# A gated mix of attention and a spectral filter on one core: the first unit's queries, keys and values are evicted into attention's own tiles

## The chip, the cores and the metric

The kernel runs on one core of a Trainium2 chip. The metric is the device time of one execution in microseconds (us). Three executions of the kernel before took 444.52, 444.55 and 444.66 us; their median, 444.55 us, is the time that the change is measured against. The core's engines each run their own list of instructions in order: PE (matrix products), DVE, ACT and POOL (elementwise work), and SP, which here only issues transfers. ACT and POOL issue transfers as well.

## The reference

The input x has 2048 positions of 640 numbers. Three things are computed from it and mixed:

```python
g = sigmoid((x * gate_w).sum(-1, keepdims=True))
# a: 32 heads of 20 numbers; position s sees positions s, s-2, ..., s-14
q, k, v = x @ wqkv, split by head
logits = q[s] . k[s - 2*w] * 20**-0.5      (w = 0..7, -1e9 before the first position)
a = (softmax(logits) weighted v) @ wo
# b: a filter in the frequency domain
b = irfft2(rfft2(x) * (w_r + 1j * w_i))
out = g * a + (1 - g) * b
```

All numbers are fp32.

## The kernel before

**Layout.** The 2048 positions lie as 128 partitions of 16 positions each (position 16p + j). Since attention reaches back in steps of two, even j (parity 0) and odd j (parity 1) are independent, and each has eight positions (jj = 0 to 7) in a partition. Position jj of a partition needs the seven positions of its parity before it, so the first seven rows that a partition uses come from the partition in front of it.

**Units.** The 32 heads go in four groups of eight, and a unit is one parity with one group: unit u = 4 * parity + group, each with 480 columns of queries, keys and values, in six blocks of 80 columns (four heads each; a and b are the two halves of a unit). The function `qkv` makes a unit: for each jj, 15 matmuls on PE (three products of split numbers over five chunks of the depth) fill one PSUM bank out of four; ACT evicts the bank with a copy of 480 columns into a tile `ev`, and for group 0 one more column into `z` for the gate; after every second jj, `store_rows` sends the pair to the tensor `qkvd` in main memory on ACT's queue. In unit 0 the weights' columns are in the order that `key_rows` undoes (query a, key a, query b, key b, value a, value b).

**Attention.** For half a unit, `fetch` loads keys (15 rows of 80, `kt`, 7 of them from the partition in front) and queries (`q`, 8 rows) from `qkvd`, and `attend` loads the values (`vt`, 15 rows). In main memory a partition's rows follow those of the partition in front, so one load of 15 rows per partition brings the overlap with it; rows before the first position were zeroed by `zero_rows`. `products` then has ACT copy two query rows into a PSUM third (`qbank`), DVE multiply them with eight keys each (`pr`) and DVE reduce them into logits (`L`); one of four such steps is on POOL except in the first units. Softmax follows on DVE, POOL and ACT, `weigh` multiplies with values on POOL (`pv`), and DVE reduces them into outputs (`o`), which go to main memory (`od`). The order of half units is 0a, 0b, 4a, 4b, 1a, 1b, 2a and so on (UNITS); the names in the trace carry that number (`pr0a`, `kt4b`).

**The filter.** `fold` turns x (`fx`) into its sums and differences by ACT, DVE or POOL; four of the eight are stored to main memory (`fd`) by ACT's queue and loaded again later. `cols` and `freq` transform (`z`, then groups of frequencies in pairs, in the order GORD = 1, 2, 3, 0, 4, ...; group 0 is special and has tables of its own, `tbfirst`), multiply with the filter and transform back (`g`, `xa`, `xc` on PE, `ab`, `xd`, `s`, `p` on DVE). `spatial`, `project_even` and `project_odd` make the output: transforms `oa` to `od`, `ha`, `hb`, and the products with wo (`woa`, `wob`).

**The order.** All calls are first recorded as a list with their dependences. A planner in the kernel file gives each a modelled length and makes an order by list scheduling forward and backward (`turns`); `order` repeats this for a list of random seeds, STEPS, each of which shakes the priorities in a part of the span. The instructions are then issued in that order, so each engine's list is fixed. Every operation is recorded by a helper, which is why all rows of the trace name the same line, L681; they are told apart by their tiles.

Of the kernel before, what the change touches and what calls it, by code (L numbers as in the profile page):

```python
# [16 lines left out]
S, D = 2048, 640  # L17
NJ = 16
HD = 20
GORD = (1, 2, 3, 0) + tuple(range(4, 16))  # L20
GC = 160
HC = 80
ROWS = 7 + 1024
# [4 lines left out]
BQ, BF = (0, 1, 2, 3), (4, 5, 6)  # L28
# [121 lines left out]
class Plan:  # L150
# [311 lines left out]

    def issue(self, tc):
        order = self.order()
        with tc.manual_schedule():
            for op in order:
                exec(*op.call)
# [29 lines left out]
)  # L497
ENGS = ("PE", "DVE", "ACT", "POOL", "SP")
BEGIN = {"PE": 0.8, "DVE": 0.5, "ACT": 0.5, "POOL": 0.5, "SP": 0.5}
ISSUE = {"SP": 0.45, "ACT": 0.42, "POOL": 1.15}  # L500
LAG = {"PE": 0.27, "DVE": 0.14, "ACT": 0.16, "POOL": 0.15}
PACKETS, RATE, LAND, LANES = (0.52e-3, 2.3e-6), 345e3, (2.3, 1.9), 8
# [36 lines left out]
class Mixer:  # L539
# [17 lines left out]
    def places(self, pp, dr, sb):  # L557
# [13 lines left out]
        def ring(*tags):  # L571
            return Ring(sb, *tags)

        def n(tag, k):
            return ring(*(f"{tag}{i}" for i in range(k)))
# [6 lines left out]
        self.evrs = {0: ring("ev0", "ev1", "pr0", "pr1"), 4: ring("e0", "e1", "ev0", "ev1")}  # L582
        self.xor = ring("raw0", "raw1", "raw2", "raw3", "raw4", "kv4", "kv5", "ya")

        self.vsr, self.mdr, self.wpr = ring("raw2"), ring("mm", "ev0", "ev1"), n("f", 3)
# [3 lines left out]
        self.wor, self.war, self.yar = ring("ya", "e1", "raw1"), ring("w2", "w3", "w4", "w0", "w1", "w5", "w6"), ring("ya")  # L589
# [13 lines left out]
    def work(self):  # L603
        p, ins = self.p, self.ins
        S = p.sp
# [16 lines left out]
        self.fetched, self.ahead = {}, None  # L622
        self.qkv(0, 0)
# [123 lines left out]
    def store_rows(self, src, u, block, jj):  # L747
        n, k = src.shape[1], src.shape[2]
        d = self.qkv_d
        to = bass.AP(  # L750
            tensor=d.tensor,
            offset=d.offset + ((6 * u + block) * ROWS + 7 + jj) * HC,
            ap=[[8 * HC, 128], [ROWS * HC, n], [1, k * HC]],
        )
        self.p.act.dma_start(to, src.rearrange("p i j c -> p i (j c)"))

    def terms_qkv(self, j, hg, c0, c1, whole):
        hi, lo = self.xT[j]
        terms = []
        for t in (0, 2, 1, 4, 3) if whole else range(5):  # L760
            x = slice(128 * t, 128 * t + 128)
            if whole:
                terms.append((self.xraw[j][:, x], self.wraw[hg, t][:, c0:c1]))
            else:
                terms += [(a[:, x], w[hg][t][:, c0:c1]) for a, w in ((hi, self.wh), (hi, self.wl), (lo, self.wh))]
        return terms

    def first_keys(self):

        p = self.p  # L770
        n = 2 * HC
        kept = self.one("ev_first", 2, 8, HC, tag="pr1")
        done = 0
        for jj in range(8):
            b = self.ps(BQ, f"qk0_{jj}")
            terms = self.terms_qkv(2 * jj, 0, 0, n, jj == 0)
            for i, (a, w) in enumerate(terms):
                p.pe.matmul(b[:, 0:n], a, w, start=(i == 0), stop=(i == len(terms) - 1))
            p.act.copy(kept[:, :, jj], b[:, 0:n].rearrange("p (i c) -> p i c", i=2))
            if jj in FIRST_STORES:  # L780
                self.store_rows(kept[:, :, done : jj + 1], 0, 0, done)
                done = jj + 1

    def qkv(self, par, hg, between=None):
        p = self.p
        u = 4 * par + hg
        b0 = 0
        c0, n = b0 * HC, 480 - b0 * HC
        for jj in range(8):
            j = 2 * jj + par  # L790
            b = self.ps(BO if u == 7 and jj > 3 else BQ, f"qkv{u}_{jj}")
            terms = self.terms_qkv(j, hg, c0, 482 if hg == 0 else 480, j == 0 and hg == 0)
            for i, (a, w) in enumerate(terms):
                p.pe.matmul(b[:, 0 : w.shape[1]], a, w, start=(i == 0), stop=(i == len(terms) - 1))
            if jj % 2 == 0:
                ev = self.evrs.get(u, self.evr).next(f"ev{u}_{jj}", 6, 2, HC)
            p.act.copy(ev[:, b0:, jj % 2], b[:, 0:n].rearrange("p (i c) -> p i c", c=HC))
            if hg == 0:
                p.act.copy(self.z[:, j : j + 1], b[:, n : n + 1])
            if jj % 2:  # L800
                self.store_rows(ev[:, b0:], u, b0, jj - 1)
            if between:
                between(jj)
# [22 lines left out]
    def attend(self, par, h, step=4):  # L826

        p, d = self.p, self.qkv_d
        V, A, G, S = p.dve, p.act, p.pool, p.sp
        u, f = 4 * par + h // 2, h % 2  # L830
        nm = f"{u}{'ab'[f]}"
# [4 lines left out]
        (S if early else self.queue("vt")).dma_start(vt.rearrange("p a b -> p (a b)"), self.key_rows(par, h, 2, 0, 15), max_dma_last_dim=PACKET)  # L836
# [125 lines left out]
    def fold(self, q):  # L962
# [44 lines left out]
        if q in STORED:  # L1007
            p.act.dma_start(self.f_d[:, q], f)
# [56 lines left out]
    def freq(self, gs):  # L1065
# [8 lines left out]
        for g in gs:  # L1074
            if g == 0:
                tb[g] = [self.one(f"tbfirst{i}", D, tag=f"raw{i}") for i in range(2)]
                for i in range(2):
                    S.dma_start(tb[g][i], ins["t_first"][:, D * i : D * i + D])
            else:
                tb[g] = mm[:, gs.index(g)]  # L1080
# [229 lines left out]
ON_ACT = ("vt", "q")  # L1310
ON_SP = ((0, 0), (0, 1), (1, 0), (1, 1))
FIRST_STORES = (3, 5, 7)
# [64 lines left out]
```

## Time and profile before

| | before |
|---|---|
| median of three runs | 444.55 us |
| the profiled execution's own time | 444.11 us |
| its span, first to last instruction | 442.3 us |
| PE busy | 429.9 us (97%) |
| DVE busy | 384.0 us (87%) |
| POOL busy | 353.5 us (80%) |
| ACT busy | 212.3 us (48%) |
| moved by the DMA queues | 95.52 MB, mean 216 GB/s |
| TensorE's granted clock | 1.00 |

A row of a group names line, engine, operation, the tile written and the tiles read, the shapes and the count, then after a bar the busy time in us and the mean of one in ns, and after another bar how long the engine had been idle just before and what ended that. A row in order of time begins with start and length in us. SPq and ACTq are the issue of a transfer on that engine. Several instructions that follow each other and are alike are merged into one row with their count. Matmuls overlap in the pipeline, so the mean of one is longer than the time between two.

### The profile page before, as it was taken

What the parts mean: (1) busy time and instruction counts of PE and PEld (TensorE: products, weight loads), DVE (VectorE), ACT (ScalarE), POOL (GpSimd) and SP (SyncE); (2) the same over time, 40 slices, a digit from 0 to 9 for tenths busy, and PEclk for the clock granted to TensorE, in tenths of its full rate; (3) what the DMA queues carried; (4) which work ended last, traced back from release to release, by engine and by line L of the source; (5) the groups of instructions that cost most, each with busy time, mean ns of one, the idle gap of its engine ahead of it and who ended that gap; (6) DMA issues with size and microseconds to landing.
All of it is one profiled execution on the core that took longest, in us unless ns stands there. A gap on an engine that the chain in (4) does not pass through costs nothing.

```text
span 442.3 us, 9192 instructions
## 1 busy us (share of the span) xinstructions
PE 429.9 (97%) x3501; PEld 371.9 (84%) x3501; DVE 384.0 (87%) x499; ACT 212.3 (48%) x551; POOL 353.5 (80%) x313
## 2 busy tenths in 40 slices
PE   8899999999999999999999998999999999999996
PEld 4788887888887888787888885888889999999996
DVE  4475189999998999799999998999999999999673
ACT  5474263332215323443334575767676777654220
POOL 1099678669999999498698996898696899499983
PEclk9999999999999999999999999999999999999999
DMA  8997998874767656998498687759843434365516
GB/s 304 380 373 241 361 346 313 276 222 124 204 171 249 193 150 195 380 310 261 141 286 239 203 252 248 221 205 309 267 134 101 120 104 150 68 114 123 115 48 131
DMA packets 83835, 95.52 MB, mean 216 GB/s; under 512 B 18104, under 2 KB 73528, under 8 KB 83792
## 3 DMA queue, kind: packets, MB, share of 16 engines
q1 hardware_dynamic: 46880, 61.83, 42.6%
q10 hardware_dynamic: 35696, 30.40, 22.4%
q0 software_dynamic: 1216, 2.71, 4.2%
q8 instruction: 27, 0.44, 0.4%
q14 instruction: 16, 0.13, 0.1%
HBM read 64.04 MB, written 30.89 MB: 215 GB/s over the span
## 4 chain that ended last, share of the span: by engine, by line
PE 58%; DVE 21%; DMA 12%; issue 4%; ACT 2%; POOL 2%; SPq 1%; ACTq 0%; DVEq 0%; POOLq 0%
PE qkv L681 26%; PE woa L681 7%; PE wob L681 7%; PE oa L681 5%; DMA qkvd<-ev 3%; PE z L681 3%; DMA f<-fd 2%; DVE xd L681 2%; DMA fx<-in_x 2%; PE ha L681 2%; PE hb L681 2%; DMA xt<-in_xT 2%; DVE s L681 2%; PE g L681 2%; DVE ab L681 2%
## 5 line engine op out<-in xcount | busy, mean ns | idle before, releaser
L681 PE MATMUL qkv<-w,xo 128*128 128x480 f32 (+1 forms) x480 | 113.1, 385 | 0.5 <-DVE fx L681 0.5
L681 PE MATMUL qkv<-w,xe 128*128 128x480 f32 (+1 forms) x465 | 106.9, 383 | 3.1 <-ACT ev L681 2.4
L681 PEld LDWEIGHTS qkv<-w,xe 128*128 128x128 f32 x465 | 86.7, 189 | 20.2 <-ACT ev L681 4.7
L681 PEld LDWEIGHTS qkv<-w,xo 128*128 128x128 f32 x480 | 89.0, 188 | 17.5 <-issue 1.7
L681 ACT COPY ev<-qkv 128x480 f32<-128x480 f32 x64 | 35.5, 561 | 77.1 <-PE qkv L681 63.4
L681 PE MATMUL woa<-wo,oT 128*128 128x320 f32 x240 | 42.2, 319 | 0.3 <-DVE oT L681 0.2
L681 PE MATMUL wob<-wo,oT 128*128 128x320 f32 x240 | 41.3, 318 | 0.0
L681 PEld LDWEIGHTS woa<-wo,oT 128*128 128x128 f32 x240 | 35.8, 188 | 2.1 <-DVE oT L681 1.3
L681 PEld LDWEIGHTS wob<-wo,oT 128*128 128x128 f32 x240 | 35.9, 188 | 1.0 <-issue 0.3
L681 POOL TENSOR_TENSOR P<-X,wp 128x642 f32<-128x642 f32 x16 | 25.0, 1562 | 5.1 <-ACT X L681 4.8
L681 POOL TENSOR_TENSOR xo<-xt,xo 128x640 fp32r<-128x640 f32 x8 | 12.3, 1570 | 19.6 <-ACT xo L681 19.6
L681 PEld LDWEIGHTS a<-bt,zg 32*128 32x128 f32 x160 | 22.1, 184 | 2.5 <-issue 1.1
L681 PE MATMUL b<-bt,zg 32*128 32x161 f32 x160 | 24.1, 300 | 0.0
L681 PE MATMUL d<-bt,zg 32*128 32x161 f32 x160 | 24.1, 300 | 0.0
L681 PE MATMUL a<-bt,zg 32*128 32x161 f32 x160 | 24.1, 300 | 0.0
L681 PE MATMUL c<-bt,zg 32*128 32x161 f32 x160 | 24.1, 300 | 0.0
L681 PE MATMUL oa<-gt,zj 32*128 32x160 f32 x160 | 23.8, 299 | 0.0
L681 PE MATMUL ob<-gt,zj 32*128 32x160 f32 x160 | 23.8, 299 | 0.0
L681 PE MATMUL oc<-gt,zj 32*128 32x160 f32 x160 | 23.8, 299 | 0.0
L681 PE MATMUL od<-gt,zj 32*128 32x160 f32 x160 | 23.8, 299 | 0.0
L681 PEld LDWEIGHTS oa<-gt,zj 32*128 32x128 f32 x160 | 21.9, 185 | 1.5 <-issue 0.7
L681 PEld LDWEIGHTS g<-mm,s 128*128 128x128 f32 x150 | 19.8, 191 | 3.2 <-ACT vs L681 1.1
(303 smaller groups left out, 1248.2 us busy)
## 6 DMA issues: line engine op xcount, KB each, us to landing
qkvd<-ev ACTq DMA_DIRECT2D x32, 480.0 KB, 5.0
wp<-in_ws SPq DMA_DIRECT2D x16, 642.0 KB, 5.3
fx<-in_x SPq DMA_DIRECT2D x8, 640.0 KB, 8.1
raw<-in_wqkv SPq DMA_DIRECT2D x15, 240.0 KB, 5.5
xt<-in_xT SPq DMA_DIRECT2D x8, 320.0 KB, 8.5
fd<-fx ACTq DMA_DIRECT2D x4, 640.0 KB, 5.4
mm<-in_t_mm SPq DMA_DIRECT2D x8, 320.0 KB, 4.7
f<-fd SPq DMA_DIRECT2D x4, 640.0 KB, 8.9
```

The lines of the kernel that those rows point to most:

```text
L681: p.dve.memset(w, 0.0)
```

## The change

Unit 0 is no longer stored and loaded. `own` takes the tiles of keys, values and queries of halves 0a and 0b before unit 0 is made, and zeroes the seven rows in front of the first partition. After each jj of unit 0, `keep` evicts the bank in six copies of 80 columns straight to row jj of the queries or row 7 + jj of the keys and values; the copies with numbers 4 and 5 (the values) are on DVE, the other four on ACT. After jj = 3 and after jj = 7 the rows made since the last time go to rows 0 to 6 of the next partition, by four transfers from tile to tile (127 partitions, 3 rows the first time and 4 the second), issued by SP. `attend` loads no values for these two halves.

The pair stores of unit 4 (odd positions, group 0) are issued by SP in place of ACT, as are the stores of the folded inputs. Group 0 of the filter moves from fourth to sixth place in GORD, and its tables to the slots `ev0` and `ev1`. The order is made anew: other seeds in STEPS, and behind them a list of moves, MOVES, each of which takes one instruction (or a group of matmuls) of one engine's list to another place in it (`moved`); `settle` then computes starting times for the lists. A function that nothing called, `first_keys`, is removed.

```diff
-GORD = (1, 2, 3, 0) + tuple(range(4, 16))
+KEEP, KEEP_DVE = (1, 4, 8), (4, 5)
+GORD = (1, 2, 3, 4, 5, 0) + tuple(range(6, 16))
...
+    def moved(self, order):
+
+        lines = {e: [op for op in order if op.eng == e] for e in ENGS}
+        base, n = {}, 0
+        for e in ENGS:
+            base[e], n = n, n + len(lines[e])
+        for k, to in zip(MOVES[::2], MOVES[1::2]):
+            e = max((e for e in ENGS if base[e] <= k), key=base.get)
+            line, k, to = lines[e], k - base[e], to - base[e]
...
     def issue(self, tc):
         order = self.order()
+        if MOVES:
+            order = self.settle(self.moved(order))
...
-        self.evrs = {0: ring("ev0", "ev1", "pr0", "pr1"), 4: ring("e0", "e1", "ev0", "ev1")}
+        self.evrs = {4: ring("e0", "e1", "ev0", "ev1")}
...
-        self.vsr, self.mdr, self.wpr = ring("raw2"), ring("mm", "ev0", "ev1"), n("f", 3)
+        self.vsr, self.mdr, self.wpr = ring("raw2"), ring("mm", "raw0", "raw1"), n("f", 3)
...
-        self.wor, self.war, self.yar = ring("ya", "e1", "raw1"), ...
+        self.wor, self.war, self.yar = ring("ya", "e1"), ...
...
+        self.own()
         self.qkv(0, 0)
...
-        self.p.act.dma_start(to, src.rearrange("p i j c -> p i (j c)"))
+        (self.p.sp if u in SP_STORES else self.p.act).dma_start(to, src.rearrange("p i j c -> p i (j c)"))
...
+    def own(self):
+
+        for f in range(2):
+            nm = f"0{'ab'[f]}"
+            kt, vt = (self.kvr.next(f"{i}t{nm}", 15, HC) for i in "kv")
+            self.fetched[0, f] = kt, vt, self.qr.next(f"q{nm}", 8, HC)
+            for to in (kt, vt):
+                self.p.dve.memset(to[0:1, 0:7], 0.0)
+
+    def keep(self, b, jj):
 
         p = self.p
+        for n, f, i in ((0, 0, 2), (1, 0, 0), (2, 1, 2), (3, 1, 0), (4, 0, 1), (5, 1, 1)):
+            to = self.fetched[0, f][i][:, jj if i == 2 else 7 + jj]
+            (p.dve.tensor_copy if n in KEEP_DVE else p.act.copy)(to, b[:, HC * n : HC * n + HC])
+        if jj + 1 in KEEP[1:]:
+            r0 = KEEP[KEEP.index(jj + 1) - 1] - 1
+            for f in range(2):
+                for to in self.fetched[0, f][0:2]:
+                    p.sp.dma_start(to[1:128, r0 : jj], to[0:127, r0 + 8 : jj + 8])
...
-            if jj % 2 == 0:
-                ev = self.evrs.get(u, self.evr).next(f"ev{u}_{jj}", 6, 2, HC)
-            p.act.copy(ev[:, b0:, jj % 2], b[:, 0:n].rearrange("p (i c) -> p i c", c=HC))
+            if u == 0:
+                self.keep(b, jj)
+            else:
+                if jj % 2 == 0:
+                    ev = self.evrs.get(u, self.evr).next(f"ev{u}_{jj}", 6, 2, HC)
+                p.act.copy(ev[:, :, jj % 2], b[:, 0:480].rearrange("p (i c) -> p i c", c=HC))
...
-            if jj % 2:
-                self.store_rows(ev[:, b0:], u, b0, jj - 1)
+            if u and jj % 2:
+                self.store_rows(ev, u, jj - 1)
...
         if q in STORED:
-            p.act.dma_start(self.f_d[:, q], f)
+            p.sp.dma_start(self.f_d[:, q], f)
...
+SP_STORES = (0, 4)
```

The lists STEPS and MOVES, which are new, are left out.

More of the change, by code (lines that the diff above doesn't have):

```diff
@@ L461, in forward, with settle @@
         return sorted(done, key=lambda o: (o.start, o.i))
+    def moved(self, order):
[6 more added lines that the diff above has]
+            line, k, to = lines[e], k - base[e], to - base[e]
+            end = k + 1
+            while e == "PE" and line[k].group and end < len(line) and line[end].group == line[k].group:
+                end += 1
+            unit = line[k:end]
+            del line[k:end]
+            to -= len(unit) * (to > k)
+            line[to:to] = unit
+        return lines
+    def settle(self, lines):
+        at, head = dict.fromkeys(ENGS, 0), {}
+        free, link, lanes, avail = dict(BEGIN), 0.0, [0.0] * LANES, {}
+        done = []
+        while len(done) < len(self.ops):
+            for e in ENGS:
+                if e not in head and at[e] < len(lines[e]):
+                    op = lines[e][at[e]]
+                    if all(q in avail for q in op.preds):
+                        head[e] = max([free[e]] + [avail[q] + self.lag(q, op) for q in op.preds])
+            e = min(head, key=head.get)
+            t, op = head.pop(e), lines[e][at[e]]
+            at[e] += 1
+            if op.size and e != "POOL":
+                lane = lanes.index(min(lanes))
+                t = max(t, lanes[lane])
+            op.start, free[e] = t, t + op.busy
+            op.end = avail[op] = free[e]
+            if op.size:
+                avail[op] = link = max(link, op.end) + op.size
+                if e != "POOL":
+                    lanes[lane] = link + op.lat
+            done.append(op)
+        return sorted(done, key=lambda op: (op.start, op.i))
     def issue(self, tc):
         order = self.order()
+        if MOVES:
+            order = self.settle(self.moved(order))
         with tc.manual_schedule():
@@ L471 @@
 STEPS = (
[25 rows of a table removed]
[26 rows of a table added]
+)
+MOVES = (
[215 rows of a table added]
 )
@@ L581, in places @@
         self.xr, self.wr, self.evr, self.rawr, self.fr = n("x", 8), ring(*WPLACES), n("ev", 2), n("raw", 5), n("f", 3)
-        self.evrs = {0: ring("ev0", "ev1", "pr0", "pr1"), 4: ring("e0", "e1", "ev0", "ev1")}
+        self.evrs = {4: ring("e0", "e1", "ev0", "ev1")}
         self.xor = ring("raw0", "raw1", "raw2", "raw3", "raw4", "kv4", "kv5", "ya")
-        self.vsr, self.mdr, self.wpr = ring("raw2"), ring("mm", "ev0", "ev1"), n("f", 3)
+        self.vsr, self.mdr, self.wpr = ring("raw2"), ring("mm", "raw0", "raw1"), n("f", 3)
         self.abr, self.Pr, self.s12r, self.Xr = ring("x0", "x1"), ring("x2", "x3"), ring("x4", "x5"), ring("raw3", "raw4")
         self.p1r = ring("x6")
-        self.wor, self.war, self.yar = ring("ya", "e1", "raw1"), ring("w2", "w3", "w4", "w0", "w1", "w5", "w6"), ring("ya")
+        self.wor, self.war, self.yar = ring("ya", "e1"), ring("w2", "w3", "w4", "w0", "w1", "w5", "w6"), ring("ya")
         self.otr, self.oTr = (ring("w7"), ring("f1", "f2")), (ring("x7"), ring("x7", "x4"))
@@ L745, in load_x, with store_rows @@
         p.chain = ""
-    def store_rows(self, src, u, block, jj):
+    def store_rows(self, src, u, jj):
         n, k = src.shape[1], src.shape[2]
@@ L751, in store_rows, with terms_qkv @@
             tensor=d.tensor,
-            offset=d.offset + ((6 * u + block) * ROWS + 7 + jj) * HC,
+            offset=d.offset + (6 * u * ROWS + 7 + jj) * HC,
             ap=[[8 * HC, 128], [ROWS * HC, n], [1, k * HC]],
         )
-        self.p.act.dma_start(to, src.rearrange("p i j c -> p i (j c)"))
-    def terms_qkv(self, j, hg, c0, c1, whole):
+        (self.p.sp if u in SP_STORES else self.p.act).dma_start(to, src.rearrange("p i j c -> p i (j c)"))
+    def terms_qkv(self, j, hg, n, whole):
         hi, lo = self.xT[j]
@@ L762, in terms_qkv @@
             if whole:
-                terms.append((self.xraw[j][:, x], self.wraw[hg, t][:, c0:c1]))
+                terms.append((self.xraw[j][:, x], self.wraw[hg, t][:, 0:n]))
             else:
-                terms += [(a[:, x], w[hg][t][:, c0:c1]) for a, w in ((hi, self.wh), (hi, self.wl), (lo, self.wh))]
+                terms += [(a[:, x], w[hg][t][:, 0:n]) for a, w in ((hi, self.wh), (hi, self.wl), (lo, self.wh))]
         return terms
-    def first_keys(self):
-        p = self.p
[L771 to L782, printed above, removed]
+    def own(self):
[6 more added lines that the diff above has]
+    def keep(self, b, jj):
+        p = self.p
+        for n, f, i in ((0, 0, 2), (1, 0, 0), (2, 1, 2), (3, 1, 0), (4, 0, 1), (5, 1, 1)):
[6 more added lines that the diff above has]
+                    p.sp.dma_start(to[1:128, r0 : jj], to[0:127, r0 + 8 : jj + 8])
     def qkv(self, par, hg, between=None):
@@ L786, in qkv @@
         u = 4 * par + hg
-        b0 = 0
-        c0, n = b0 * HC, 480 - b0 * HC
         for jj in range(8):
@@ L791, in qkv @@
             b = self.ps(BO if u == 7 and jj > 3 else BQ, f"qkv{u}_{jj}")
-            terms = self.terms_qkv(j, hg, c0, 482 if hg == 0 else 480, j == 0 and hg == 0)
+            terms = self.terms_qkv(j, hg, 482 if hg == 0 else 480, j == 0 and hg == 0)
             for i, (a, w) in enumerate(terms):
                 p.pe.matmul(b[:, 0 : w.shape[1]], a, w, start=(i == 0), stop=(i == len(terms) - 1))
-            if jj % 2 == 0:
-                ev = self.evrs.get(u, self.evr).next(f"ev{u}_{jj}", 6, 2, HC)
-            p.act.copy(ev[:, b0:, jj % 2], b[:, 0:n].rearrange("p (i c) -> p i c", c=HC))
+            if u == 0:
[4 more added lines that the diff above has]
+                p.act.copy(ev[:, :, jj % 2], b[:, 0:480].rearrange("p (i c) -> p i c", c=HC))
             if hg == 0:
-                p.act.copy(self.z[:, j : j + 1], b[:, n : n + 1])
-            if jj % 2:
-                self.store_rows(ev[:, b0:], u, b0, jj - 1)
+                p.act.copy(self.z[:, j : j + 1], b[:, 480:481])
+            if u and jj % 2:
+                self.store_rows(ev, u, jj - 1)
             if between:
@@ L835, in attend @@
         kt, vt, q = self.fetched.pop((par, h), None) or self.fetch(par, h)
-        (S if early else self.queue("vt")).dma_start(vt.rearrange("p a b -> p (a b)"), self.key_rows(par, h, 2, 0, 15), max_dma_last_dim=PACKET)
+        if (par, h) not in ((0, 0), (0, 1)):
+            (S if early else self.queue("vt")).dma_start(vt.rearrange("p a b -> p (a b)"), self.key_rows(par, h, 2, 0, 15), max_dma_last_dim=PACKET)
         L = self.Lr.next(f"L{nm}", 8, 4, 8)
@@ L1075, in freq @@
             if g == 0:
-                tb[g] = [self.one(f"tbfirst{i}", D, tag=f"raw{i}") for i in range(2)]
+                tb[g] = [self.one(f"tbfirst{i}", D, tag=f"ev{i}") for i in range(2)]
                 for i in range(2):
@@ L1310 @@
 ON_ACT = ("vt", "q")
+SP_STORES = (0, 4)
 ON_SP = ((0, 0), (0, 1), (1, 0), (1, 1))
-FIRST_STORES = (3, 5, 7)
 POOL_PR = {(p, h): (6,) for p in range(2) for h in range(8) if (p, h) not in ((0, 0), (0, 1), (1, 0))}
```

266 rows, old and new, of tables (MOVES, STEPS) are left out of this document.

## The prediction

> **What bounds the kernel now.** I read the page first, its engine shares and its 40 slices of 11 us each.
>
> ```profile
> span 442.3 us, 9192 instructions
> PE 429.9 (97%) x3501; PEld 371.9 (84%) x3501; DVE 384.0 (87%) x499; ACT 212.3 (48%) x551; POOL 353.5 (80%) x313
> PE   8899999999999999999999998999999999999996
> DVE  4475189999998999799999998999999999999673
> POOL 1099678669999999498698996898696899499983
> DMA  8997998874767656998498687759843434365516
> ```
>
> PE is busy nearly everywhere and only 442.3 - 429.9 = 12.4 us are idle. DVE has one deep hole, in the slice from 44 to 55 us (digit 1), and after it hardly any until the end. To see what a microsecond is worth where, I cut the span into stages. The columns are length, then busy time of PE, PEld, DVE, ACT and POOL, clock, DMA share and GB/s.
>
> ```profile
> 0.00:44.00 44.00, 40.97 (x167) 31.99 (x168) 23.94 (x47) 23.24 (x50) 22.86 (x26) 1.00 0.93 324
> 44.00:60.00 16.00, 16.00 (x75) 13.76 (x74) 5.24 (x4) 5.62 (x18) 9.53 (x11) 1.00 1.06 367
> 60.00:140.00 80.00, 79.34 (x362) 67.11 (x361) 77.48 (x67) 28.03 (x81) 68.06 (x59) 1.00 0.76 238
> 140.00:240.00 100.00, 98.14 (x741) 82.59 (x739) 95.96 (x89) 38.23 (x104) 87.32 (x66) 1.00 0.74 230
> 240.00:340.00 100.00, 96.85 (x1016) 82.65 (x1014) 94.96 (x160) 66.00 (x172) 85.14 (x71) 1.00 0.69 219
> 340.00:442.30 102.30, 98.55 (x1148) 93.75 (x1148) 86.45 (x136) 51.17 (x129) 80.59 (x83) 1.00 0.46 111
> ```
>
> From 60 to 340 us DVE is idle for 280 - (77.48 + 95.96 + 94.96) = 11.6 us, PE for 280 - (79.34 + 98.14 + 96.85) = 5.7 us: two engines that are nearly full, and after 340 us PE alone. A busy PE is not a PE at its peak, so I compared PE's group times between 240 and 340 us with undisturbed runs of the same shapes in the chain of waits (start, length, what).
>
> ```profile
> L681 PE MATMUL g<-mm,s 128*128 128x128 f32 x150 | 21.2, 277 | 0.6 <-DVE s L681 0.6
> L681 PE MATMUL wob<-wo,oT 128*128 128x320 f32 x75 | 12.6, 319 | 0.0
> L681 PE MATMUL woa<-wo,oT 128*128 128x320 f32 x75 | 12.3, 316 | 0.1
> ```
>
> ```profile
> 70.61 61.90 PE qkv L681 x281
> 284.22 2.01 PE g L681 x18
> 414.65 2.20 PE wob L681 x15
> ```
>
> Undisturbed, a g takes 2.01/18 = 0.112 us and a wo 2.20/15 = 0.147 us; here they take 21.2 - 150 x 0.112 = 4.4 us and 24.9 - 150 x 0.147 = 2.9 us more. With the 3.15 us of idle that is some **10.4 us that PE loses between 240 and 340 us**, in a stage where DVE is 95% busy and the idle time of g is put down to it. That loss can be had if DVE's work arrives earlier; the matmuls themselves cannot.
>
> **Term 1, the front: ACT is no longer held by a store.** ACT's and PE's order of time around 20 us:
>
> ```profile
> 14.82 0.57 ACT L681 COPY ev<-qkv 128x480 f32<-128x480 f32 x1
> 15.27 0.74 ACT L681 CAST xe<-st 128x640 fp32r<-128x640 f32 x1
> 20.51 0.39 ACTq L681 DMA_DIRECT2D qkvd<-ev  x1
> 20.94 0.16 ACT L681 COPY z<-qkv 128x1 f32<-128x1 f32 x1 [4.92 <-DMA xt<-in_xT]
> 21.00 0.56 ACT L681 COPY ev<-qkv 128x480 f32<-128x480 f32 x1
> 21.61 7.97 PE L681 MATMUL qkv<-w,xe 128*128 128x482 f32 x35 [1.20 <-ACT ev L681]
> ```
>
> The pair of rows that the first store carries was evicted by 15.4 us. The store went out at 20.51, after a wait put down to an input tile's landing; behind it on ACT stood the next eviction, and PE ran out of free banks for 1.20 us. The change has no store of unit 0 at all and gives those of unit 4 to SP, so this hold goes: **-1.2 us**. Next late at that place are the input tiles themselves; bounds 0 and 1.2.
>
> [...]
>
> **Term 2: the first attention starts earlier on DVE.** The way now, in order of time on ACT, SP and DVE, with the landing times (last number) from the list of DMA issues:
>
> ```profile
> 40.07 0.58 ACT L681 COPY ev<-qkv 128x480 f32<-128x480 f32 x1
> 40.68 0.37 ACTq L681 DMA_DIRECT2D qkvd<-ev  x1
> 45.18 0.64 SPq L681 DMA_DIRECT2D kt0a<-qkvd  x1
> 52.34 0.97 ACT L681 COPY qbank<-q0a 128x160 f32<-128x160 f32 x3
> 53.35 2.89 DVE L681 TENSOR_TENSOR pr0a<-kt0a,qbank 128x1280 f32<-128x1280 f32 x2 [13.09 <-ACT qbank L681]
> ```
>
> ```profile
> 40.68 3.93 DMA qkvd<-ev
> ```
>
> ```profile
> kt0a<-qkvd SPq DMA_DIRECT2D x1, 600.0 KB, 7.1
> vt0b<-qkvd SPq DMA_DIRECT2D x1, 600.0 KB, 13.2
> ot<-od SPq DMA_DIRECT2D x8, 320.0 KB, 3.0
> ```
>
> Eviction, store (3.93), load (7.1), copy of the queries, product. The change leaves eviction and one transfer, of four rows by 127 partitions by 320 bytes, 163 KB for each tile. The trace shows no such transfer; the bounds are the 3.0 us of the fastest loads above and the 13.2 us of vt0b. I take the store's 3.93, as it starts at the same moment and is issued as a short one. The last eviction takes four copies on ACT in place of one, of some 0.23 us each (worked out below), so it ends at 40.07 + 0.92 = 41.0; the landing is then at 44.9, and with 0.3 us for a query copy DVE's first product starts at 45.2 in place of 53.35: **8.1 us earlier**. At 13.2 us of landing it would start at 54.5, and nothing is gained.
>
> These 8.1 us go into a DVE that is full from 60 to 340 us, so its stream moves as one. What is late next are the keys of unit 4, the heads that follow:
>
> ```profile
> 69.48 0.38 SPq L681 DMA_DIRECT2D kt4a<-qkvd  x1
> 79.26 1.43 DVE L681 TENSOR_TENSOR pr4a<-kt4a,qbank 128x1280 f32<-128x1280 f32 x1
> ```
>
> ```profile
> kt4a<-qkvd SPq DMA_DIRECT2D x1, 600.0 KB, 3.8
> ```
>
> They land at 69.48 + 3.8 = 73.3 and would be wanted at 79.26 - 8.1 = 71.2. The 2.1 us between are covered if DVE sums values of unit 0 first, and lost if not. What DVE gains, PE can use only out of the 10.4 us that it loses between 240 and 340. I take half, as other causes (ACT's turns, the order of the groups) stand behind the rest: **-5.2 us**, bounds 0 and 8.1.
>
> **What is added, and its cover.** ACT's eviction of unit 0, eight copies of 480 columns, becomes 32 copies of 80, DVE takes 16.
>
> ```profile
> L681 ACT COPY ev<-qkv 128x480 f32<-128x480 f32 x9 | 5.0, 565 | 0.7 <-PE qkv L681 0.7
> L681 ACT COPY z<-qkv 128x1 f32<-128x1 f32 x9 | 1.5, 163 | 10.8 <-PE qkv L681 5.9 <-DMA xt<-in_xT 4.9
> L681 DVE RECIPROCAL g<-g 128x16 f32<-128x16 f32 x1 | 0.2, 245 | 0.0
> ```
>
> Between 163 ns for 1 column and 565 for 480, 80 columns are 163 + 79 x 402/479 = 229 ns. 32 x 0.229 - 8 x 0.565 = 2.8 us more on ACT, which is idle for 20.8 of the first 44 us: cost nothing, and at most 2.8 if that cover is gone, since a late eviction holds a bank. DVE's copies lie between the 0.245 us of 16 columns (a reciprocal) and the 0.565 of ACT's 480 columns; 80 is nearest to the first, so 0.25: 16 x 0.25 = 4 us in a stretch where DVE is idle for 20.1 us: nothing, bound 4. [...]
>
> The DMA queues lose unit 0's stores (8 tiles of 245,760 bytes, 1.97 MB) and its six loads (3.11 MB), and gain 1.14 MB (four tiles of 7 rows by 127 partitions by 320 bytes): 3.9 MB less, 11 us at the 324 to 367 GB/s of the first 60 us. I credit nothing, since PE is busy for all of 44 to 60 us; bound -0.7, PE's idle time from 60 to 140. On SP's queue six loads go; eight transfers, four stores of unit 4 and four of folded inputs come. They are short issues (0.4 to 0.6 us), but each waits for its data on an in-order queue, with weight and key loads behind. I take nothing, since SP issues nothing for most of the time, and price the other case below. ACT's queue loses 12 issues of 0.37 us, under work that is not bound. Group 0 of the spectrum moves from fourth to sixth and changes its slots: the same instructions, nothing; its own wait today bounds it by 0.6.
>
> The whole order on all engines is written anew by a longer search. No row can price that. I take zero; it can give no more than the losses above and can cost what the last rival costs.
>
> **The sum.** 442.3 - 1.2 - 5.2 = 435.9 us of span. The profiled execution took 444.11 us, 1.8 beyond its span, so 437.7; the median of the runs is 444.55, 0.44 more: **438.1 us**, 1.5% less.
>
> **The rivals.**
>
> *PE takes all of it, chance 0.12.* DVE's earlier stream and the new order free the 10.4 us whole: 444.55 - 1.2 - 10.4 = 432.9. For it: the loss is in the stage in which DVE is 95% busy. Against it: 10.4 is more than DVE's 8.1.
>
> *Hidden anyway, 0.20.* PE is 97% busy, and the DVE gain is spent waiting for unit 4's keys, or the halo lands as late as vt0b; only the front is left: 443.35, between 442.5 and 444.8. For it: no slice of PE is low. Against it: the idle time and the stretched groups above.
>
> *SP becomes the bound, slower, 0.16.* The place is SP between 30 and 75 us. It now holds unit 4's stores, each behind an eviction, and the transfers behind unit 0's; the weights of the next unit and unit 4's keys are queued behind. Its waits for weight slots today (sum, times, longest):
>
> ```profile
> SPq L681 <- POOL w L681: 31.5, 11, 7.3
> ```
>
> If a hold of 7.3 us is passed on to the weights, PE has about one tile of other work in hand, 15 x 61.90/281 = 3.3 us, and idles for 4.0; the keys are late by as much and term 2 is gone: 444.55 - 1.2 + 4.0 = 447.4. It decides from a hold of 4.5 us (3.3 + 1.2). Against it: the weights are issued well ahead now and stores of unit 4 have four tiles of their own.
>
> **How the numbers follow.** The forecast has 0.52, with its own range from 434.5 to 441.5 (term 2 between about 9 and 2). The range for 8 in 10 goes from 433.5 to 446.5: it leaves out the lower part of the first rival and the upper half of the last. Differences under 0.2% (0.9 us) cannot be told from no change here. Faster: 0.52 + 0.12 + half of 0.20 = 0.74; same 0.10; slower 0.16.
>
> **What would show it.** Term 1: no store ahead of an eviction on ACT near 20 us, PE's idle time of 1.20 gone. Term 2: the first pr0a near 45 us, and PE's groups g and wo between 240 and 340 us nearer to 0.112 and 0.147 us. Wrong it would be if pr0a starts no sooner than 53, if DVE gets a new hole between 75 and 100 us for unit 4's keys, if PE idles between 45 and 75 us for weights, or if DVE is early but PE's total loss stays.

## The result

The changed kernel takes **482.87 us** (median, 481.05 to 483.53), the kernel before beside it 444.61: 1.085 times, interval 1.0825 to 1.0875. The forecast of 438.1 us, its range up to 446.5 and its sign are all wrong. The chance for slower was 0.16, and that rival's price, 447.4, was too small by 35.5 us.

The page of the changed kernel, its engine shares and its 40 slices, now of 12 us each; PEclk is the granted TensorE clock in tenths:

```profile
span 481.8 us, 9220 instructions
PE 435.9 (90%) x3501; PEld 378.0 (78%) x3501; DVE 385.7 (80%) x519; ACT 211.3 (44%) x575; POOL 354.6 (74%) x313
PE   5998829059999999999999998899899999999997
DVE  5483099016999999989999899889899999998572
...
PEclk9999868569999999999999999999999999999999
DMA  8952042667793977499987687737676333265534
```

The slices of DVE and DMA say where: from 48 us on all engines thin out, and at 110 us they are full again. DMA falls to 2 and 0 tenths between 36 and 60 us, where it stood at 7 to 9 before. The stages cut as in the prediction (length, busy PE, PEld, DVE, ACT, POOL, clock, DMA share, GB/s):

```profile
0.00:44.00 44.00, 39.06 (x156) 30.84 (x157) 26.85 (x64) 23.97 (x75) 16.52 (x20) 1.00 0.73 251
44.00:60.00 16.00, 12.90 (x52) 10.64 (x51) 0.00 (x0) 1.49 (x5) 8.19 (x9) 0.89 0.08 28
60.00:140.00 80.00, 52.33 (x222) 43.99 (x221) 52.66 (x48) 19.54 (x62) 43.31 (x41) 0.81 0.61 193
140.00:240.00 100.00, 100.00 (x658) 85.06 (x656) 96.12 (x87) 36.75 (x99) 94.93 (x72) 1.00 0.77 234
240.00:340.00 100.00, 96.15 (x967) 81.46 (x970) 92.21 (x124) 51.05 (x138) 81.73 (x68) 1.00 0.71 224
```

PE idles for 27.7 us between 60 and 140, where it had idled for 0.7. DVE does nothing from 44 to 60. The DMA share there is 0.08 at 28 GB/s. One of 16 engines is a share of 0.0625, so for 16 us little more than one engine is at work on average while DVE stands still. In order of time, DVE, PE, ACT and SP of the changed kernel:

```profile
61.18 1.49 DVE L947 TENSOR_TENSOR pr0a<-kt0a,qbank 128x1280 f32<-128x1280 f32 x1 [20.27 <-DMA kt0a<-kt0a]
```

```profile
49.67 12.14 PE L947 MATMUL qkv<-w,xo 128*128 128x482 f32 x47 [3.10 <-ACT z L947]
70.60 7.99 PE L947 MATMUL qkv<-w,xo 128*128 128x482 f32 x26 [8.78 <-ACT z L947]
...
102.05 8.12 PE L947 MATMUL qkv<-w,xe 128*128 128x480 f32 x28 [18.89 <-POOL w L947]
```

```profile
48.51 0.59 ACT L947 CAST w<-raw 128x480 fp32r<-128x480 f32 x1 [4.13 <-DMA raw<-in_wqkv]
...
65.35 0.30 ACT L947 COPY qbank<-q0b 128x160 f32<-128x160 f32 x1 [15.73 <-DVE pr0a L947]
...
95.05 0.59 ACT L947 CAST w<-raw 128x480 fp32r<-128x480 f32 x1 [18.22 <-DMA raw<-in_wqkv]
```

```profile
36.89 5.43 SPq L947 DMA_DIRECT2D raw<-in_wqkv  x1
...
43.57 5.21 SPq L947 DMA_DIRECT2D kt0a<-kt0a  x1
48.88 5.49 SPq L947 DMA_DIRECT2D kt0b<-kt0b  x1
54.47 9.74 SPq L947 DMA_DIRECT2D fd<-fx  x2
69.67 0.38 SPq L947 DMA_DIRECT2D fx<-in_x  x1
70.11 3.78 SPq L947 DMA_DIRECT2D vt0b<-vt0b  x2
73.98 5.87 SPq L947 DMA_DIRECT2D raw<-in_wqkv  x2
```

The chain reads backwards. The first product waits 20.27 us for the rows that the key tile gets from the partition in front. ACT has the next query copy at the head of its list, which waits for that product's place in PSUM (15.73 us); behind it stand the evictions of unit 4, so PE runs out of banks for 8.78 us. Several of SP's issues take 5.2 to 5.5 us in place of 0.4 to 0.6 while those transfers are in flight, so the loads of the next weights go out late and land late. That makes the other two waits of PE: at 48.51 ACT has waited 4.13 us to convert a weight chunk, with evictions behind it, and PE has no bank for 3.10 us; at 95.05 it has waited 18.22 us, and PE idles 18.89 us for the weights themselves.

### The profile page after: what moved, and what is told of

Its sections match the earlier page's. It is cut to its first block, busy times and chain, and to the rows that moved or that the text cites. A ratio compares the mean times of both kernels' runs of the same rounds, so it can differ in the third digit from the quotient of the medians.

```text
span 481.8 us, 9220 instructions
## 1 busy us (share of the span) xinstructions
PE 435.9 (90%) x3501; PEld 378.0 (78%) x3501; DVE 385.7 (80%) x519; ACT 211.3 (44%) x575; POOL 354.6 (74%) x313
## 5 line engine op out<-in xcount | busy, mean ns | idle before, releaser
L947 PE MATMUL qkv<-w,xo 128*128 128x480 f32 (+1 forms) x480 | 115.5, 394 | 11.9 <-ACT z L947 11.9
L947 PEld LDWEIGHTS qkv<-w,xe 128*128 128x128 f32 x465 | 88.5, 191 | 34.5 <-POOL w L947 19.7
L947 PEld LDWEIGHTS qkv<-w,xo 128*128 128x128 f32 x480 | 92.0, 194 | 29.7 <-ACT z L947 12.7
L947 ACT COPY ev<-qkv 128x480 f32<-128x480 f32 x56 | 31.2, 557 | 63.8 <-PE qkv L947 60.7
L947 PE MATMUL wob<-wo,oT 128*128 128x320 f32 x240 | 42.6, 319 | 0.0
L947 POOL TENSOR_TENSOR fm<-fx 128x320 f32<-128x320 f32 x3 | 2.6, 861 | 36.4 <-DMA fx<-in_x 36.4
L947 ACT CAST oT<-oTp 128x384 fp32r<-128x384 f32 (+1 forms) x32 | 13.4, 430 | 24.7 <-PE woa L947 12.9
L947 ACT CAST w<-raw 128x480 fp32r<-128x480 f32 x15 | 8.9, 593 | 34.6 <-DMA raw<-in_wqkv 30.7
```

The source lines that it names most:

```text
L947: p.dve.memset(w, 0.0)
```

## The experiments

Unless said otherwise an experiment edits the changed kernel and leaves the order on every engine as it was. "Split version" means the first.

### The transfers split in 112 and 15 partitions

```diff
+    def halo(self, dst, src):
+        for a, b in ((0, 112), (112, 127)):
+            self.nc.sync.dma_start(dst[a:b], src[a:b])
...
                     p.sp.dma_start(to[1:128, r0 : jj], to[0:127, r0 + 8 : jj + 8])
+                    p.ops[-1].call[1]["fn"] = self.halo
```

> The changed kernel in its own order, but each of the eight transfers to the next partition is issued as two, of 112 and of 15 partitions, in the same place of SP's list. Theory A (a transfer over 127 partitions runs on one DMA engine and takes tens of us in a row; everything behind waits for it): the last of the eight lands within 5 us of its issue, the first pr0a starts near 45 us in place of 61, PE's idle 3.1, 8.8 and 18.9 us before 105 us go, and the time falls by their sum and about 6 us of slowed clock, from 482.9 to between 438 and 446. Theory B (SP's order is at fault: unit 4's stores and the folded inputs' stores wait there and hold the weights' loads): PE still waits for weights between 75 and 105 us, and the time stays above 465. Theory C (the new order of all engines is at fault): no single wait dominates, above 465 as well.

445.48 us (before beside it 444.38; ratio 1.0026, 1.0014 to 1.0038). The first product, and the landing of the second transfer of that tile's 112 partitions from the list of issues:

```profile
41.42 1.49 DVE L947 TENSOR_TENSOR pr0a<-kt0a,qbank 128x1280 f32<-128x1280 f32 x1 [1.44 <-DMA kt0a<-kt0a]
```

```profile
kt0a<-kt0a SPq DMA_DIRECT2D x1, 140.0 KB, 2.3
```

The stages from 44 to 140 us:

```profile
44.00:60.00 16.00, 16.00 (x74) 13.75 (x73) 15.70 (x12) 5.43 (x19) 14.38 (x16) 1.00 0.87 265
60.00:140.00 80.00, 80.00 (x368) 68.78 (x367) 71.00 (x64) 26.26 (x77) 72.83 (x60) 1.00 0.74 227
```

2.3 us to landing, and the product 19.8 us earlier. PE has no idle time between 44 and 140. Of the 38.1 us between the spans (481.8 and 443.7), the three waits are 30.8, and PE's busy time falls by 6.4 (from 435.9 to 429.5). I put this to the clock, as an estimate: between 60 and 140 us a matmul takes 80.00/368 = 0.217 us at a granted clock of 1.00, and took 52.33/222 = 0.236 at 0.81. Theory A holds; 0.9 us is left for all other causes in those 38 us. The time is still not under that of the kernel before, which is a question of its own, below.

### The transfers over 128 partitions, and none at all

```diff
+    def halo(self, dst, src):
+        whole = [bass.AP(tensor=v.tensor, offset=v.offset - first * v.ap[0][0], ap=[[v.ap[0][0], 128], *v.ap[1:]])
+                 for v, first in ((dst, 1), (src, 0))]
+        self.nc.sync.dma_start(*whole)
```

> The changed kernel with the eight transfers over 128 partitions in place of 127, each into its own partition: same rows, same queue, same places, 1 partition more, but the shift by one partition is left out, so the rows in front hold other data. Theory A: the 128 partitions spread over all DMA engines, time as the split version within 1 us, 438 to 446. If the place or the size of the transfers, or their way from tile to tile, were slow in itself: as the changed kernel, about 483.

445.46 us (ratio 1.0032, 1.0014 to 1.005): one transfer each, same queue and place, one partition more, and 37 us less. So neither the way from tile to tile nor the small size was slow, but the count 127.

```diff
                 self.p.dve.memset(to[0:1, 0:7], 0.0)
+                self.p.ops[-1].call[1]["a"] = (to[0:128, 0:7], 0.0)
...
                     p.sp.dma_start(to[1:128, r0 : jj], to[0:127, r0 + 8 : jj + 8])
+                    p.ops[-1].call[1]["fn"] = lambda dst, src: None
```

> The changed kernel without the eight transfers: the rows in front are zeroed in all partitions in place of the first, so the overlap between partitions is left out; all else stands at its place in the same order. It is the floor of what a quick transfer could bring. Theory A: 0 to 3 us under the split version. Theory B and C: above 465.

445.85 us (1.0038, 1.002 to 1.0057). The places of the transfers stay empty here and the first rows of the tiles are zeros in all partitions. Without any transfer nothing is gained over the split version (445.48): the split transfers cost this kernel nothing that can be told.

### The transfers split in 122 and 5 partitions

```diff
-        for a, b in ((0, 112), (112, 127)):
+        for a, b in ((0, 122), (122, 127)):
```

> As the split version, but split in 122 and 5 partitions: 122 is twice a prime, 61. If a transfer runs on as many engines as divide its partitions (up to 16), the large part runs on two: half the time of the 127, some 3 us of packets for each in place of 5.6 to 7, with the eight of them in a row 25 us in place of 50; time between the split version and the changed kernel, 447 to 465. If 127 is slow for another reason (an odd count, the last partition): as the split version, 445.

459.13 us (1.0329, 1.0304 to 1.0354). The first product starts between the two others:

```profile
49.19 1.49 DVE L947 TENSOR_TENSOR pr0a<-kt0a,qbank 128x1280 f32<-128x1280 f32 x1 [9.08 <-DMA kt0a<-kt0a]
```

Partitions of the large part, start of the first product, time: 112, 41.4 us, 445.5 us; 122, 49.2, 459.1; 127, 61.2, 482.9. An odd count or the last partition is ruled out, as 122 is even and leaves the last five out. That the divisors of the count decide is the assumption this run was built on: its time lies in the range expected from it, but three counts do not show it in general. The trace does not name the engine of a packet, but it keeps the start and length of each. A packet of 1280 bytes took 0.057 to 0.058 us on average in each of the kernels with 127, 122 and 128 partitions; what differed is how many passed at a time. Over 127 partitions the 127 packets of the last transfer into `kt0a` follow each other from 53.85 to 60.61 us: 7.18 us of packets in 6.76 us, one at a time. With 122 partitions the packets of the last transfers into both key tiles go two at a time (14.51 us of packets from 44.44 to 51.83). Over 128 partitions the 128 packets into `kt0a` pass from 38.49 to 39.08 us, twelve at a time. The DMA share (last number but one) in windows inside the first and the last of these stretches agrees, 0.07 against 0.88 of 16 engines:

```profile
54.00:60.00 6.00, 6.00 (x28) 5.11 (x27) 0.00 (x0) 0.00 (x0) 1.10 (x2) 0.95 0.07 24
```

```profile
38.50:39.00 0.50, 0.50 (x4) 0.41 (x4) 0.50 (x2) 0.50 (x3) 0.50 (x1) 1.00 0.88 312
```

### The same transfers on ACT's queue

```diff
+                    p.ops[-1].call[1]["fn"] = self.nc.scalar.dma_start
```

> The changed kernel with its transfers over 127 partitions as they are, but issued on ACT's queue in place of SP's. If what costs is that the weights' loads stand behind the slow transfers in SP's queue: the weights land in time, PE's idle 18.9 us goes, 445 to 462. If what costs is that the keys themselves come late (and ACT or DVE wait for them in order): pr0a near 60 us as in the changed kernel and PE idle by 10 us or more for want of evictions, 462 to 483.

479.6 us (1.0789). The first product starts at 61.80, as late as on SP. The weights are not what PE waits for in its two long waits here; ACT itself is held by the issue of these transfers (rows of ACT's queue and of PE):

```profile
37.31 6.70 ACTq L947 DMA_DIRECT2D kt0b<-kt0b  x1
...
75.18 7.30 ACTq L947 DMA_DIRECT2D vt0a<-vt0a  x1
```

```profile
51.35 17.91 PE L947 MATMUL qkv<-w,xo 128*128 128x482 f32 x68 [9.91 <-ACT kt0b L947]
83.83 7.85 PE L947 MATMUL qkv<-w,xo 128*128 128x482 f32 x26 [14.57 <-ACT z L947]
```

So the late weights were one of the ways in which the delay reached PE. Here ACT's held issues take their place, and 35 of the 38 us stay. What the way over the weights costs by itself is not shown by this run.

### Without the list of moves, with slow and with quick transfers

```diff
-MOVES = (
-    3917, 3919, 3379, 3381, 775, 796, 4013, 4015, 2971, 2969, 3206, 3211, 3789, 3791, 427, 434, 3098, 3090,
...
-)
+MOVES = ()
```

> The changed kernel with its transfers over 127 partitions on SP, new seeds, without the moves. If the loss is the transfers' own and not their meeting with this order: 30 to 45 us above the same order with split transfers, 472 to 487. If the moves made it worse than it had to be: 450 to 470.

477.1 us (1.0734, 1.0693 to 1.0774) with the transfers over 127 partitions.

> The split version with the new seeds but without the list of moves. My prediction counted the order at zero. If the moves carry a gain: above the split version by 3 to 20 us (the old seeds without moves gave 466). If the late start of the first product came with the moves, it starts at 4.05 us here.

441.55 us with split transfers (0.9933, 0.9912 to 0.9955). In the same order, the transfers alone make 35.5 us of difference (36.8 against the repeat below). They do not need the moves to do harm. The moves themselves do not help on the chip: with them the split version stood at 445.48. The first product of all starts at 4.05 here, 7.25 there, and 3.2 of these 3.9 us are that late start, as the experiment on the first loads shows.

> The split version with the new seeds and without the moves once more, beside the next kernel on the same chip and with more runs: 441 to 442.5 if the moves bring nothing on the chip, under the kernel before by 0.5% or more.

440.3 us (0.9915, 0.9888 to 0.9942). This repeats the kernel above and comes out a little under what was expected. Its time is the shortest of all by its median, 0.85% under the kernel before.

### The first loads in the order of need

In the split version the first product waits for a weight chunk:

```profile
7.25 1.95 PE L947 MATMUL qkv<-st 128*128 128x482 f32 x2 [3.25 <-DMA st<-in_w]
```

ACT's list there begins with the chunks 2, 4, 0, in the kernel before with 0, 2, 4. The first product reads chunk 0.

```diff
+        act, sp = lines["ACT"], lines["SP"]
+        act[0:3], sp[0:2] = sorted(act[0:3], key=lambda op: op.i), sorted(sp[0:2], key=lambda op: op.i)
+        act[3], act[4] = act[4], act[3]
         return lines
```

> The split version with one more edit: ACT's first three loads and SP's first two go out in the order of need, as in the kernel before (first the weight chunk and the 128 columns of x that the first product reads), and the first two conversions on ACT change places with them. In the new order that chunk is ACT's third load and lands at 7.1 us, and the first product starts at 7.25 us in place of 4.05. If PE is what bounds from there on: 3.2 us less than the split version, 441.5 to 443, which is under the kernel before. If DVE's or another chain bounds and the late start is hidden behind it: within 1 us of the split version.

442.26 us (0.9956, 0.9941 to 0.9971), 3.2 us under the split version, and the first product is back at 4.05:

```profile
4.05 1.86 PE L950 MATMUL qkv<-st 128*128 128x482 f32 x2
```

A start that is 3.2 us late goes through to the end whole; no slack hides it. DVE's first `pr4a` came 3.2 us sooner as well (75.93 to 72.69), so this alone does not tell PE from DVE as the bound. This is the 1.1 us by which the split version is above the kernel before, and more.

### The order by itself

The changed program with split transfers, the seeds of the kernel before and no moves:

```diff
 STEPS = (
-    2501007, 2501012, 2501014, 2501019, 2501023, 2501027, 2501028, 2501043, 2501046, 2501051, 2501065, 2501069,
...
+    1002, 1007, 1010, 1016, 1017, 1018, 1022, 1031, 1035, 1036, 1048, 1052, 1055, 1059, 1061, 1074, 1076, 1113, 1124,
...
+MOVES = ()
```

> The changed kernel with the transfers split in 112 and 15 partitions, planned with the seeds of the kernel before and without the list of moves; eviction into attention's tiles, stores on SP and the place of group 0 stay. What it is above the split version in the new order is what the order brings. My prediction counted the order at zero: then within 2 us of the split version. If the order carries the gain: 445 to 452.

It took 466.19 us (1.0476, 1.0439 to 1.0512), more than either expectation.

The kernel before without its seeds:

```diff
-STEPS = (
-    1002, 1007, 1010, 1016, 1017, 1018, 1022, 1031, 1035, 1036, 1048, 1052, 1055, 1059, 1061, 1074, 1076, 1113, 1124,
...
-)
+STEPS = ()
```

> The kernel before without its list of seeds, so in the planner's first order. It prices the order by itself, which my prediction put at zero: if the search of the order is worth as much as the split version with old seeds suggested, 455 to 475; if the order hardly matters, 445 to 448.

It took 453.06 us (1.0193, 1.0146 to 1.024). So the order that the seeds make is worth some 9 us in the kernel before, and for the changed program the range over three ways of making it is 440 to 466 us. For the changed list of operations, the seeds found for the old list give a time some 25 us longer than its own seeds do. Whether they are better or worse there than no seeds is not shown: no run of the changed program goes without seeds.

### Unit 4's stores back on ACT

In the split version without moves:

```diff
         (self.p.sp if u in SP_STORES else self.p.act).dma_start(to, ...)
+        if u in SP_STORES:
+            self.p.ops[-1].call[1]["fn"] = self.nc.scalar.dma_start
```

> The same kernel without moves, but unit 4's four stores are issued on ACT's queue at the places where SP had them. By my term 1 (a store on ACT that has to wait holds the evictions behind it): ACT idle before a store by some us and PE idle in 50 to 75 us, 443 to 447. If another issuing engine saves only the time of the issue, four times 0.4 us on an engine that is half idle: within 0.7 us of the kernel without this edit.

440.72 us (0.992, 0.9895 to 0.9945), beside 440.3 for the same kernel with these stores on SP: no difference that can be told. Issues on ACT between 45 and 85 us took 0.37 to 0.40 us each and none shows a wait of a microsecond or more ahead of it.

## Why the prediction was wrong

**What bounds.** Right as far as it is shown: in the mended kernel without moves (split transfers, new seeds) PE is busy for 428.0 of 438.3 us, and a late start of 3.2 us came through in full.

**Term 1 (-1.2).** Right in the trace of the new order: no version with the new seeds has the wait at 21 us. In the mended kernel without moves PE runs through that place:

```profile
11.74 16.37 PE L731 MATMUL qkv<-w,xe 128*128 128x482 f32 x72
```

But unit 4's stores on ACT, which the prediction named beside unit 0's, are no part of it: moved back to ACT they change nothing that can be told (440.72 against 440.3 us). PE's idle time before 44 us fell by only 0.7, as a wait of 1.06 us for a weight chunk came in at 7.85.

**Term 2 (-5.2): the step that failed.** "I take the store's 3.93" priced the transfer by the landing of a store over 128 partitions, and the bound of 13.2 us by a load over 128. Size, way and issue were considered; the number of partitions entered as bytes alone. Over 127 partitions the packets went one at a time, at a DMA share of 0.07: the last rows for `kt0a` were issued at 43.57 us and their last packet ended at 60.61, 17 us later in place of 3.93. The bound was wrong in kind as well: it let a late landing only undo a gain ("nothing is gained"), while slow transfers in a row held SP's list, ACT's list and so PE. "They are short issues (0.4 to 0.6 us)" failed with it: issues on SP took up to 7.0 us. The measured price is 37 us for 127 against 128 partitions.

The rest of term 2 can be read from the mended versions, those with split transfers, and the mechanism is right in its first half only. The products did start early: 39.95 in place of 53.35 (13.4 us, where 8.1 was forecast). A part of this was handed back at the next heads. Rows of DVE, ACT and SP in the mended kernel without moves, then landings:

```profile
39.95 2.88 DVE L731 TENSOR_TENSOR pr0a<-kt0a,qbank 128x1280 f32<-128x1280 f32 x2 [1.11 <-DMA kt0a<-kt0a]
...
67.08 0.25 DVE L731 RECIPROCAL g<-g 128x16 f32<-128x16 f32 x1 [2.82 <-ACT g L731]
...
73.90 1.49 DVE L731 TENSOR_TENSOR pr4a<-kt4a,qbank 128x1280 f32<-128x1280 f32 x1 [3.23 <-ACT qbank L731]
```

```profile
73.24 0.63 ACT L731 COPY qbank<-q4a 128x160 f32<-128x160 f32 x2 [1.40 <-DMA q4a<-qkvd]
```

```profile
67.67 0.38 SPq L731 DMA_DIRECT2D kt4a<-qkvd  x1
68.10 0.50 SPq L731 DMA_DIRECT2D q4a<-qkvd  x1
```

```profile
kt4a<-qkvd SPq DMA_DIRECT2D x1, 600.0 KB, 4.7
q4a<-qkvd SPq DMA_DIRECT2D x1, 320.0 KB, 5.1
```

Unit 4's keys land at 67.67 + 4.7 = 72.4, one us sooner than in the kernel before, and the first product with them starts at 73.90 in place of 79.26. At this place DVE keeps 5.4 of the 13.4 us. The prediction named these keys as what would be late next, and then sized the loss at 2.1 us. The wait that ends last here is another one: the queries of the same half, issued right behind the keys, land at 68.10 + 5.1 = 73.2, and ACT's copy of them and then DVE's product start with that. ACT's late work on the gate (2.82 us before 67.08) is the other part of the hole. No run removes either wait by itself.

The lead comes back behind the hole. The next heads, unit 1, start 8.4 us sooner than before; first the kernel before, then the mended one:

```profile
113.17 1.48 DVE L681 TENSOR_TENSOR pr1a<-kt1a,qbank 128x1280 f32<-128x1280 f32 x1
```

```profile
104.79 1.48 DVE L731 TENSOR_TENSOR pr1a<-kt1a,qbank 128x1280 f32<-128x1280 f32 x1
```

So behind the hole DVE had about the lead that the prediction gave it, 8.1 us (the eviction and the new order together). What failed in the second half of term 2 is what PE makes of it: the lead did not arrive in PE's waits between 240 and 340 us. The mended kernel without moves, same stages:

```profile
span 438.3 us, 9229 instructions
...
0.00:44.00 44.00, 41.68 (x172) 32.67 (x173) 32.97 (x70) 26.21 (x81) 23.29 (x27) 1.00 0.88 298
60.00:140.00 80.00, 80.00 (x368) 68.68 (x367) 72.00 (x64) 27.94 (x78) 73.37 (x61) 1.00 0.79 233
140.00:240.00 100.00, 99.15 (x805) 83.89 (x807) 94.91 (x90) 40.80 (x107) 90.49 (x70) 1.00 0.79 247
240.00:340.00 100.00, 96.39 (x974) 83.46 (x967) 94.52 (x158) 65.13 (x169) 82.43 (x70) 1.00 0.67 212
```

PE's idle time there is 3.6 us, against 3.15 before. Nor did the groups come nearer to their undisturbed times, as the prediction's sign asked:

```profile
L731 PE MATMUL g<-mm,s 128*128 128x128 f32 x150 | 20.5, 276 | 0.2 <-DVE s L731 0.2
L731 PE MATMUL woa<-wo,oT 128*128 128x320 f32 x90 | 15.1, 319 | 1.9 <-DVE oT L731 1.9
L731 PE MATMUL wob<-wo,oT 128*128 128x320 f32 x87 | 14.6, 318 | 0.0
```

A g takes 20.5/150 = 0.137 us (0.141 before, 0.112 undisturbed), a wo 29.7/177 = 0.168 (0.166 before, 0.147 undisturbed). The 4.0 us between the spans (442.3 and 438.3) lie elsewhere: 0.7 less idle before 44, 0.7 between 60 and 140, 1.0 between 140 and 240, 1.9 less busy time (429.9 to 428.0), 0.2 at the end, and 0.5 lost in that stage. Which part of this belongs to the eviction and which to the new seeds stays open: the order cannot be held while the operations change. That the mended kernel's 440.3 us lies inside the range given with the forecast (434.5 to 441.5) is therefore no proof of term 2; its 5.2 us are not found where it put them.

**What was added.** The copies of 80 columns take 0.23 us on ACT, as worked out, and 0.24 on DVE (0.25 taken). In the new order the cover was there. In the order from the old seeds it was not quite: there PE waits for these copies three times before 44 us, 0.34 to 0.76 us each.

**The order at zero.** Wrong. The order is worth 9 us in the kernel before, some 25 us lie between two orders of the changed one, and the new one began with a loss of 3.2 us in the list of ACT's first loads. The bound "can cost what the last rival costs" (447.4, some 3 us) was too narrow.

**The rival on the other side** (SP becomes the bound) had the place right, SP between 30 and 75 us with weights and keys behind it, and the wrong cause. The hold came from the transfers themselves, not from their waits for evictions, and it had no such limit as the 7.3 us taken from SP's waits for weight slots.

## What to carry to other kernels

Look at the number of partitions of a transfer before its size: packets over 127 partitions went one at a time, over 122 two, over 128 twelve, and a transfer split in 112 and 15 cost one more issue of some 0.7 us. A slow transfer on an in-order queue must be priced by all that stands behind it on every engine, not by the gain that it undoes. Where an order of instructions was searched for one list of operations, a change of that list puts the value of the search at stake (466 against 440 us here), and its first few loads are worth reading one by one.

## What the runs showed of the hardware

Issues were held while transfers over 127 partitions were in flight, those of other transfers too: SP's issues of 0.4 to 0.6 us took up to 7.0 us (a load of weights at 80.58), ACT's up to 7.3 with these transfers on its own queue. In the kernel before no issue took more than 2.3 us. So here such a transfer cost the issuing engine and all that it issued next. And the granted TensorE clock was lower in the stage with PE's long waits, 0.81 as a mean between 60 and 140 us of the changed kernel, against 1.00 there in the split version; going by PE's busy time, 435.9 against 429.5 us, I estimate that this cost some 6.4 us beside the 30.8 us of the waits.
